# Chunked attention into a Swish feed-forward on one Trainium2 core: one more unit on each transfer-transpose path, and the order of the blocks around it

## The chip, the core and the metric

The kernel runs on one core of a Trainium2 chip. The core has five engines that run side by side: TensorE (PE, with its weight loads shown apart as PEld), VectorE (DVE), ScalarE (ACT), GpSimd (POOL, which here mostly issues loads) and SyncE (SP, which here issues stores and transposing transfers). Each engine works through its own list of instructions in order; an instruction that waits holds up all that stand behind it on that engine. The metric is the device time of one execution in microseconds (us).

## The reference

Attention within chunks of 64 tokens (8 batches, 8 heads, 576 tokens, head width 64), then a feed-forward with a Swish of its own slope for every hidden column:

```python
scores = scale * np.matmul(q_c, k_c.transpose(0, 1, 2, 4, 3))   # chunks of 64 x 64
attn = np.exp(scores - max); attn = attn / (sum + 1e-09)
x = np.matmul(attn, v_c)  -> [4608, 512]
h = x @ w_in                                                    # [512, 2048]
g = h * (1.0 / (1.0 + np.exp(-beta * h)))
out = g @ w_out                                                 # [2048, 512]
```

## The kernel before, in words

The 4608 tokens are cut into 18 **units** of 256 tokens and 9 **blocks** of two units each. Blocks 0 and 1 take units 0 to 3, block 2 takes units 4 and 5, block 3 takes 6 and 7, block 4 takes 8 and 9, and so on.

**Attention, unit by unit.** `load_qk` and `load_v` (lines 98 to 123) load q, k and v with GpSimd, cast to half precision. `emit_T` (line 152) turns q and k so that the head width lies on the partitions. For units below `XU` that is done by two DVE transposes (line 164), kT and qT. From `XU` on it is two transposing transfers issued by SP (line 159), and the loads then use another layout (line 106: two loads of 128 rows for q and two for k where line 112 has one each of 256 rows). `emit_T` also lets GpSimd issue loads up to four units ahead, and those wait for a free buffer of q and k (four of each). `emit_sc` (line 210) makes the scores: 64 small matmuls (line 232) for units below `XU`, 32 (line 219) from there on, then one ACT exponential. `emit_pv` (line 244) multiplies by v, `emit_norm` (line 301) divides on DVE and leaves x of half a unit, called x16. x must then be turned as well: `emit_xt_pe` (line 324) does half a unit with four PE transposes (line 329) and an ACT copy (line 333); `emit_xt_dma` (line 346) does it with a transposing transfer on SP (line 348). In the kernel before, units 0 to 5 go by the PE and units 6 to 17 by transfers.

**Feed-forward, block by block.** `emit_m(j, m)` makes one of the 16 column groups of the hidden layer of block j: four matmuls of 512 columns into a PSUM tile hps (line 372), an ACT tanh into sg (line 384), and a DVE instruction that makes gt from both (line 360). It reads the turned x of all four half units of its block. The second matrix product uses seven products of half size for four quarters; `emit_prod(j, p, t)` is half t of product p, eight matmuls of 256 columns (line 585), accumulated in one of two PSUM tiles; products 1, 6, 7, 4 go to the first and 2, 5, 3 to the second. The finished quarter is copied by ACT (line 602) or added by DVE (line 605). DVE also makes the sums that these products need: `emit_sum` (line 436) from gt, `emit_wt` (line 427) from the weights. In block j the core runs the first layer of block j and the products of block j-1, with the attention of later units between.

In blocks 6 to 8 the first layer too uses seven products for three quarters of its columns: `emit_q` (line 491), whose results are copied (line 503, ACT), added (line 506, DVE), put through Silu (`emit_q_silu`, line 513, three parts of two ACT instructions) and scaled into gt (`emit_q_scale`, line 527, DVE). The other four groups are `emit_m` with a Silu (line 381) and `emit_mg` (line 356, DVE).

**PSUM.** In block 2 the pool of four `p` buffers holds the two accumulators of block 1's products, so that two are left for hps: an `emit_m` needs the gt of the one two places before it. From block 3 on the accumulators are two tiles of their own, ya and yb.

**Order.** The order is written by hand: for every block a list of items (place, priority, what) is sorted by place and then priority (lines 738 to 801), and each engine gets its instructions in that order. An item's place is a share of the block.

Of the kernel before, what the change touches and what calls it, by code (L numbers as in the profile page):

```python
# [8 lines left out]
FP32 = mybir.dt.float32  # L9
# [6 lines left out]
def kernel(  # L16
# [59 lines left out]

    blocks = [(u, 2) for u in range(0, NU, 2)]
    NB = len(blocks)
    XU = 9
    WV = 8  # L80
    QB = 6
    unit_block = {}
# [469 lines left out]
    def emit_prod(j, p, t):  # L552
        last = j == NB - 1
        if p == 1 and t == 0:
            if j == 1:
                a = [ps_p[0].tile([128, 512], FP32, tag="p", name="acc") for _ in range(2)]
            else:
                a = [ps_y[0].tile([128, 512], FP32, tag=n, name=n) for n in (("yb", "ya") if last else ("ya", "yb"))]
            if last:
                a = [[ps_p[0].tile([128, 512], FP32, tag="p", name="acc") for _ in range(2)], a]  # L560
            acc_t[j] = a
        g = gt_t[j]
        acc = acc_t[j][0 if p in (1, 6, 7, 4) else 1]
        acc, dst = (acc[t][:, 0:256],) * 2 if last else (acc, acc[:, 256 * t:256 * t + 256])
        c0 = t * 128
        for kk in range(8):
            lhsT = {
                1: lambda: g[:, kk, c0:c0 + 128],
                2: lambda: g[:, 8 + kk, c0:c0 + 128],
                3: lambda: sm[3][:, kk, c0:c0 + 128],  # L570
                4: lambda: g[:, 8 + kk, 256 + c0:256 + c0 + 128],
                5: lambda: sm[0][:, kk, c0:c0 + 128],
                6: lambda: sm[1][:, kk, c0:c0 + 128],
                7: lambda: sm[2][:, kk, c0:c0 + 128],
            }[p]()
            rhs = {
                1: lambda: w_at(0, kk, 0),
                2: lambda: w_at(1, kk, 0),
                3: lambda: w_at(1, kk, 1),
                4: lambda: wt[3][:, kk, :],  # L580
                5: lambda: wt[0][:, kk, :],
                6: lambda: wt[1][:, kk, :],
                7: lambda: wt[2][:, kk, :],
            }[p]()
            nc.tensor.matmul(  # L585
                out=dst,
                lhsT=lhsT,
                rhs=rhs,
                start=(p in (1, 2, 5) and kk == 0 and (t == 0 or last)),
                stop=(kk == 7 and (t == 1 or last)),  # L590
                skip_group_check=True,
            )
        if t == 0 and not last:
            return
        flush_stores()
        r, c, how = {1: (0, 0, "copy"), 2: (0, 0, "add"), 6: (0, 1, "copy"), 5: (1, 1, "copy"),
                     7: (1, 1, "add"), 3: (0, 1, "add"), 4: (1, 0, "copy")}[p]
        key = (j, r, c, t if last else None)
        if how == "copy":
            o = osl_p[0].tile([128, 256], FP32, name="osl") if last else osb_p.tile([128, DM], FP32, tag="osb", name="osb")  # L600
            oq_t[key] = o
            nc.scalar.copy(out=o, in_=acc)  # L602
        else:
            o = oq_t[key]
            nc.vector.tensor_tensor(out=o, in0=acc, in1=o, op=ALU.add)
        if p in (2, 7, 3, 4):
            late.append(key)
# [6 lines left out]
    with tc.manual_schedule():  # L614
# [104 lines left out]
        def att_items(u, a0, w):  # L719
            it = [(a0, 2, ("sc", u)), (a0 + 0.36 * w, 3, ("pv", u)), (a0 + 0.361 * w, 3, ("norm", u, 0)),  # L720
                  (a0 + (0.42 if u >= WV else 0.50) * w, 3, ("norm", u, 1))]
            if u >= WV:
                it.append((a0 + (0.45 * w if u == 9 else 0.005), 3, ("T", u + 3)))
            return it

        ATT = {2: ((6, 0.36, 0.27), (7, 0.60, 0.27)),
               3: ((8, 0.01, 0.30), (9, 0.28, 0.30), (10, 0.66, 0.33)),
               4: ((11, 0.02, 0.33), (12, 0.35, 0.33), (13, 0.68, 0.33)),
               5: ((14, 0.02, 0.30), (15, 0.30, 0.30), (16, 0.58, 0.30), (17, 0.86, 0.28))}
# [8 lines left out]
        for j in range(1, NB):  # L738
# [6 lines left out]
            items = []  # L745
            if j == 1:
                items += [(0.04 * m, 0, ("h", m)) for m in range(8)]
                items += [(0.32 + 0.0850 * (m - 8), 0, ("m", m)) for m in range(8, KFF)]
                items += [(0.30, 3, ("T", 4)), (0.52, 2, ("sc", 4)), (0.70, 2, ("pv", 4)), (0.71, 3, ("norm", 4, 0)),
                          (0.80, 3, ("norm", 4, 1)), (0.56, 3, ("Th", 5, "kT")), (0.63, 3, ("Th", 5, "qT"))]  # L750
                items += [(c, 3, ("wt", i)) for i, c in ((1, 0.47),)]
            else:
                m0 = {2: 0.36, 4: 0.09}.get(j, 0.02)
                if j < QB:
                    items += [(m0 + (1 - m0) * m / KFF, 0, ("m", m)) for m in range(KFF)]
                else:
                    lane = LANE[2 if j == QB else j == NB - 1]
                    cost = [1 if it[0] == "q" and it[2] == 3 else 2 for it in lane]
                    for n, it in enumerate(lane):
                        c, e, f = (0.98 * sum(cost[:n + d]) / sum(cost) for d in (0, 1, 2))  # L760
                        items.append((c, 0, it))
                        if it[0] == "m":
                            items.append((c + 0.04, 3, ("mg", it[1])))
                        elif it[0] == "last":
                            pass
                        elif it[2] == 2:
                            if j == NB - 1 and it[1] == 3:
                                f = e
                            items += [(f - 0.002, 2, ("qs", it[1], 2)), (f - 0.001, 2, ("qs", it[1], 1)),
                                      (f + 0.03, 3, ("qt", it[1], 0))]  # L770
                        elif it[2] == 3:
                            items += [(c + 0.001, 2, ("qs", it[1], 0)), (c + 0.04, 3, ("qt", it[1], 1))]
                    if j == QB:
                        items.append((0.01, 6, ("open",)))
                        items += [(0.011+0.001*n, 6, ("tx", QB, n)) for n in range(4)]
                    if j + 1 < NB:
                        items += [(0.70 + 0.06 * n, 5, ("tx", j + 1, n)) for n in range(4)]
# [5 lines left out]
                    for i, c in ((2, 0.72), (0, 0.80), (1, 0.86)):  # L783
                        items.append((c, 4, ("pre", i)))
                for i in range(4):
                    s0 = (0.01, 0.08, 0.25, 0.33)[i] if j == 2 else 0.005 + 0.07 * i
                    if j >= QB:
                        s0 = (0.08, 0.15, 0.33, 0.48)[i] if j == QB else (0.003, 0.10, 0.33, 0.48)[i]
                    items.append((s0, 4, ("sum", i)))
                if j == 2:  # L790
                    items += [(c, 3, ("wt", i)) for i, c in ((2, 0.36), (3, 0.55))]
                    items += [(0.03, 0, ("sc", 5)), (0.06, 2, ("xp", 4, 0)), (0.09, 2, ("xp", 4, 1)),
                              (0.17, 2, ("pv", 5)), (0.18, 3, ("norm", 5, 0)), (0.19, 3, ("norm", 5, 1)),
                              (0.24, 3, ("T", 6)), (0.53, 3, ("T", 7)), (0.60, 3, ("T", 8)), (0.61, 3, ("T", 9)), (0.80, 3, ("T", 10)),
                              (0.30, 2, ("xp", 5, 0)), (0.32, 2, ("xp", 5, 1))]
                for jw, i, c, d in ((3, 2, 0.10, 0.22), (4, 1, 0.21, 0.22), (4, 3, 0.10, 0.22)):
                    if jw == j:
# [4 lines left out]
            for _, _, it in items:  # L802
# [13 lines left out]
                    emit_pv(it[1], (0, 1) if len(it) == 2 else (it[2],))  # L816
                elif it[0] == "norm":
                    emit_norm(it[1], it[2])
                    if it[1] not in (4, 5):
                        emit_xt_dma(it[1], it[2])  # L820
                elif it[0] == "xp":
                    emit_xt_pe(it[1], it[2])
# [68 lines left out]
```

## Time and profile before

| what | before |
|---|---|
| time, median of 3 runs (lowest to highest) | 276.55 us (276.26 to 276.83) |
| the profiled execution's own time | 276.39 us |
| its span, first to last instruction | 274.6 us |
| TensorE's granted clock | full in all slices |
| transposing transfer of x (line 348), 24 of them, median issue to landing | 6.6 us |
| transposing transfers of k and of q (line 159), 9 of each, median | 9.3 and 9.8 us |
| block 2, from its first product to the first of block 3 | 62.90 to 94.83 us |

The difference between the profiled execution's time and its span, 1.8 us, lies around the program's instructions. Times of single events below are counted from the start of the span. In the lists of instructions a row has the start, the time, the engine, the line, the operation, the tile written and the tiles read, how many instructions are merged, and in brackets how long the engine had been idle and what ended it.

### The profile page before, as it was taken

Reading aid. Unit: us, or ns where it says so; the run is one execution under the profiler, and the core shown is the slowest. Engines: PE = TensorE matmul, PEld = TensorE weight load, DVE = VectorE, ACT = ScalarE, POOL = GpSimd, SP = SyncE. Lnnn points to the kernel's source line nnn. Section 1 sums busy time; section 2 is a strip of 40 time slices with the busy share of each in tenths; the row PEclk is TensorE's granted clock in tenths of the full one; section 3 lists DMA queues with packets and bytes.
Section 4 is the critical chain, followed back from the end, with each engine's and each line's share of the span. In section 5 each row is a group of like instructions: output and inputs, shape, how many; then the busy total and the mean of one; then the engine's idle time right before and its main releaser. Section 6 shows DMA issues by size and latency. Waiting matters only on the chain.

```text
span 274.6 us, 7824 instructions
## 1 busy us (share of the span) xinstructions
PE 266.6 (97%) x3237; PEld 184.8 (67%) x3237; DVE 210.0 (76%) x394; ACT 166.8 (61%) x300; POOL 95.2 (35%) x122
## 2 busy tenths in 40 slices
PE   7799999999999999999999999999999999999995
PEld 2575445847665666666666666668887887778874
DVE  3567666899998598678977896759896977777961
ACT  2388416976664565556655655576768495858721
POOL 8954478489639935333445200000000000000000
PEclk9999999999999999999999999999999999999999
DMA  9999999999999999999999999853111102110223
GB/s 137 170 195 203 190 181 187 235 171 172 173 149 168 171 174 153 176 146 146 158 153 195 133 137 197 183 147 80 41 54 60 41 0 79 38 41 1 78 79 115
DMA packets 141763, 36.43 MB, mean 133 GB/s; under 512 B 125856, under 2 KB 141216, under 8 KB 141728
## 3 DMA queue, kind: packets, MB, share of 16 engines
q0 software_dynamic: 99136, 18.10, 83.3%
q1 hardware_dynamic: 42592, 17.84, 35.7%
q8 instruction: 25, 0.41, 0.6%
q14 instruction: 10, 0.08, 0.1%
HBM read 36.71 MB, written 9.44 MB: 168 GB/s over the span
## 4 chain that ended last, share of the span: by engine, by line
PE 78%; DVE 10%; ACT 5%; issue 3%; DMA 2%; POOL 0%; DVEq 0%; ACTq 0%; POOLq 0%
PE hps L372 28%; PE ya L585 14%; PE yb L585 11%; PE ops L397 5%; PE acc L585 5%; PE qx L484 4%; PE qz L484 4%; DVE gt L360 3%; ACT hq L513 3%; DMA sm<-in_k_dram 2%; DVE gt L527 2%; PE sc L232 2%; DVE sm L436 1%; PE sc L219 1%; PE x L270 1%
## 5 line engine op out<-in xcount | busy, mean ns | idle before, releaser
L372 PE MATMUL hps<-xt,win 128*128 128x512 f16 (+1 forms) x488 | 106.5, 355 | 0.5 <-DVE gt L360 0.3
L384 ACT ACTIVATE sg<-hps,bt 128x512 f32<-128x512 f32 (+1 forms) x111 | 69.3, 635 | 35.0 <-PE hps L372 32.6
L360 DVE SCALAR_TENSOR_TENSOR gt<-sg,hps 128x512 f16<-128x512 f32 (+1 forms) x111 | 67.6, 617 | 27.7 <-ACT sg L384 26.8
L372 PEld LDWEIGHTS <-win 128*128 128x128 f16 x488 | 46.2, 98 | 32.1 <-issue 1.0
L585 PEld LDWEIGHTS <-sm 128*128 128x128 f16 x512 | 49.4, 98 | 12.0 <-issue 0.3
L585 PEld LDWEIGHTS <-gt 128*128 128x128 f16 x384 | 36.9, 98 | 10.3 <-DVE gt L527 0.8
L120 POOL DMA_DIRECT2D vbig<-in_v_dram x40 | 34.0, 864 | 24.8 <-DMA ku<-in_k_dram 7.4
L585 PE MATMUL ya<-wt,sm 128*128 128x256 f16 x200 | 25.9, 273 | 0.0
L527 DVE TENSOR_SCALAR gt<-hq,rb 128x512 f16<-128x512 f32 x36 | 16.3, 483 | 8.4 <-ACT hq L513 7.2
L106 POOL DMA_DIRECT2D qu<-in_q_dram x20 | 17.1, 872 | 14.1 <-DVE qT L164 5.8
L106 POOL DMA_DIRECT2D ku<-in_k_dram x20 | 17.1, 880 | 12.2 <-DMA qu<-in_q_dram 7.8
L513 ACT ACTIVATE hq<-hq,bs 128x256 f32<-128x256 f32 (+1 forms) x36 | 19.2, 612 | 1.8 <-DVE hq L506 1.8
L436 DVE TENSOR_TENSOR sm<-gt 128x2048 f16<-128x2048 f16 (+1 forms) x17 | 19.7, 1156 | 0.3
L602 ACT COPY osb<-ya 128x512 f32<-128x512 f32 x18 | 10.6, 589 | 8.6 <-PE ya L585 7.9
L484 PEld LDWEIGHTS <-ws 128*128 128x128 f16 x144 | 14.1, 98 | 2.4 <-issue 0.7
L241 ACT ACTIVATE et<-sc 128x1024 f16<-128x1024 f32 (+1 forms) x10 | 8.3, 852 | 11.4 <-PE sc L232 11.4
L397 PE MATMUL ops<-wout,gt 128*128 128x512 f16 x64 | 14.7, 379 | 0.0
L585 PE MATMUL yb<-wout,gt 128*128 128x256 f16 x104 | 13.9, 273 | 0.3 <-DVE gt L527 0.2
L585 PE MATMUL yb<-wt,sm 128*128 128x256 f16 x104 | 13.5, 273 | 0.1
L503 ACT COPY hq<-qx 128x512 f32<-128x512 f32 x18 | 10.6, 587 | 4.9 <-PE qx L484 4.8
L585 PE MATMUL ya<-wout,gt 128*128 128x256 f16 x104 | 13.5, 273 | 0.0
L585 PE MATMUL yb<-wout,sm 128*128 128x256 f16 x104 | 13.5, 273 | 0.0
(99 smaller groups left out, 355.7 us busy)
## 6 DMA issues: line engine op xcount, KB each, us to landing
out_dram<-osb SPq DMA_DIRECT2D x32, 256.0 KB, 2.8
vbig<-in_v_dram POOLq DMA_DIRECT2D x32, 128.0 KB, 7.5
qu<-in_q_dram POOLq DMA_DIRECT2D x18, 128.0 KB, 12.5
ku<-in_k_dram POOLq DMA_DIRECT2D x18, 128.0 KB, 14.6
win<-in_moe_w_in_dram POOLq DMA_DIRECT2D x8, 256.0 KB, 8.7
wout<-in_moe_w_out_dram POOLq DMA_DIRECT2D x4, 512.0 KB, 13.2
qu<-in_q_dram POOLq DMA_DIRECT2D x5, 256.0 KB, 7.0
ku<-in_k_dram POOLq DMA_DIRECT2D x5, 256.0 KB, 7.1
```

The costliest lines, as they stand in the source:

```text
L106: nc.gpsimd.dma_start(out=tv[off:off + n, sp], in_=src[b, :, s:s + n, :].rearrange("h p d -> p h d"),)
L120: nc.gpsimd.dma_start(out=vbig[off:off + n, i % NV, :, 0:D], in_=v[b, :, s:s + n, :].rearrange("h p d -> p h d"),)
L360: nc.vector.scalar_tensor_tensor(out=gt_t[j][:, m, c0:c0 + n], in0=sg[:, 0:n], scalar=1.0, in1=hps[:, 0:n], op0=ALU.add, op1=ALU.mult,)
L372: nc.tensor.matmul(out=hps[:, 0:n], lhsT=w_in16[m // 2][:, kk, (m % 2) * 128:(m % 2) * 128 + 128], rhs=xr[:, c0 // CH:(c0 + n) // CH, 2 * ...
L384: nc.scalar.activation(out=sg[:, 0:n], in_=hps[:, 0:n], func=ACTF.Tanh, scale=bt[:, m:m + 1])
L397: nc.tensor.matmul(out=ops, lhsT=gt_t[j][:, kk, t * 128:(t + 1) * 128], rhs=w_out16[kk // 4][:, kk % 4, :], start=(kk == 0), stop=(kk == K ...
L436: nc.vector.tensor_tensor(out=sm[i][:, lo:hi, :], in0=a, in1=b, op=op)
L484: nc.tensor.matmul(out=dst[:, s, :], lhsT=lhsT, rhs=rhs, start=(p in (1, 2, 5) and s == 0 and kk == 0), stop=(s == 1 and kk == 1), skip_gr ...
L503: nc.scalar.copy(out=o, in_=z if p == 5 else x)
L513: nc.scalar.activation(out=o, in_=src, func=ACTF.Silu, scale=bs[:, m:m + 1])
L527: nc.vector.tensor_scalar(out=gt_t[j][:, m, :], in0=hq[:, b].rearrange("p c q -> p (c q)"), scalar1=rb[:, m:m + 1], scalar2=None, op0=ALU. ...
L585: nc.tensor.matmul(out=dst, lhsT=lhsT, rhs=rhs, start=(p in (1, 2, 5) and kk == 0 and (t == 0 or last)), stop=(kk == 7 and (t == 1 or last ...
```

## The change

Five edits, all in the order or in which path a unit takes.

1. `XU` is 8 in place of 9: q and k of unit 8 are loaded in the other layout and turned by two transfers on SP, and its scores take 32 matmuls.
2. x of unit 4 is turned by two transfers behind its two norms; the two items `xp 4` are gone from block 2.
3. Orders in blocks 1 and 2. In block 1 only `T 4` moves, ahead of the half group `h 7`. In block 2: `sc 5` goes behind the second half of product 1; `sum 3` goes behind `m 0` and `sc 6`, `wt 2` behind `m 1`, `wt 3` behind `sc 7`; `T 8` goes ahead of `m 4` and `T 7` (it stood behind `sc 7`); `pv 7` with the first norm of unit 7 goes behind `prod 3 0` and `m 9`, and the second norm behind `m 10` and `prod 3 1`.
4. In blocks 6 to 8 the Silu parts of a q group: part 2 goes one item of the lane earlier, and in blocks 6 and 7 the last group's parts 2 and 1 go ahead of `m 3`, its first scaling ahead of `prod 4 1`.
5. The two accumulators change places from block to block (yb first in even blocks, ya first in odd ones), where before only the last block had them the other way.

```diff
-    XU = 9
+    XU = 8
...
-                a = [ps_y[0].tile([128, 512], FP32, tag=n, name=n) for n in (("yb", "ya") if last else ("ya", "yb"))]
+                a = [ps_y[0].tile([128, 512], FP32, tag=n, name=n) for n in (("ya", "yb") if j % 2 else ("yb", "ya"))]
...
-        ATT = {2: ((6, 0.36, 0.27), (7, 0.60, 0.27)),
+        ATT = {2: ((6, 0.36, 0.27), (7, 0.60, 0.36)),
...
-                items += [(0.32 + 0.0850 * (m - 8), 0, ("m", m)) for m in range(8, KFF)]
-                items += [(0.30, 3, ("T", 4)), (0.52, 2, ("sc", 4)), (0.70, 2, ("pv", 4)), (0.71, 3, ("norm", 4, 0)),
-                          (0.80, 3, ("norm", 4, 1)), (0.56, 3, ("Th", 5, "kT")), (0.63, 3, ("Th", 5, "qT"))]
+                items += [(0.34 + 0.0820 * (m - 8), 0, ("m", m)) for m in range(8, KFF)]
+                items += [(0.26, 3, ("T", 4)), (0.52, 2, ("sc", 4)), (0.70, 2, ("pv", 4)), (0.715, 3, ("norm", 4, 0)),
+                          (0.75, 3, ("norm", 4, 1)), (0.56, 3, ("Th", 5, "kT")), (0.63, 3, ("Th", 5, "qT"))]
...
-                            if j == NB - 1 and it[1] == 3:
+                            if it[1] == 3:
                                 f = e
-                            items += [(f - 0.002, 2, ("qs", it[1], 2)), (f - 0.001, 2, ("qs", it[1], 1)),
+                            items += [(e - 0.002, 2, ("qs", it[1], 2)), (f - 0.001, 2, ("qs", it[1], 1)),
                                       (f + 0.03, 3, ("qt", it[1], 0))]
...
-                    s0 = (0.01, 0.08, 0.25, 0.33)[i] if j == 2 else 0.005 + 0.07 * i
+                    s0 = (0.01,0.08,0.28,0.36)[i] if j == 2 else 0.005 + 0.07 * i
...
-                    items += [(c, 3, ("wt", i)) for i, c in ((2, 0.36), (3, 0.55))]
-                    items += [(0.03, 0, ("sc", 5)), (0.06, 2, ("xp", 4, 0)), (0.09, 2, ("xp", 4, 1)),
+                    items += [(c, 3, ("wt", i)) for i, c in ((2, 0.40), (3, 0.60))]
+                    items += [(0.07, 2, ("sc", 5)),
                               (0.17, 2, ("pv", 5)), (0.18, 3, ("norm", 5, 0)), (0.19, 3, ("norm", 5, 1)),
-                              (0.24, 3, ("T", 6)), (0.53, 3, ("T", 7)), (0.60, 3, ("T", 8)), (0.61, 3, ("T", 9)), (0.80, 3, ("T", 10)),
+                              (0.24, 3, ("T", 6)), (0.53, 3, ("T", 7)), (0.50, 3, ("T", 8)), (0.61, 3, ("T", 9)), (0.80, 3, ("T", 10)),
                               (0.30, 2, ("xp", 5, 0)), (0.32, 2, ("xp", 5, 1))]
...
-                    if it[1] not in (4, 5):
+                    if it[1] != 5:
                         emit_xt_dma(it[1], it[2])
```

## The prediction

> **What bounds the kernel.** I read the page's busy times first, then busy times by stretch, then which PE starts were late.
>
> ```profile
> span 274.6 us, 7824 instructions
> PE 266.6 (97%) x3237; PEld 184.8 (67%) x3237; DVE 210.0 (76%) x394; ACT 166.8 (61%) x300; POOL 95.2 (35%) x122
> ...
> DMA  9999999999999999999999999853111102110223
> ```
>
> PE is the bound: only what takes PE time away, or a moment in which PE waits, can shorten the span. The transfer engines are full for the first 25 of 40 slices (to 172 us). By stretch (total, then busy us of PE, PEld, DVE, ACT, POOL):
>
> ```profile
> 51.60:75.40 23.80, 23.54 (x427) 15.64 (x428) 23.44 (x41) 16.81 (x29) 18.24 (x22) 1.00 2.07 177
> 75.40:96.50 21.10, 20.65 (x309) 12.80 (x294) 16.51 (x30) 11.74 (x17) 16.71 (x21) 1.00 2.18 162
> 96.50:185.00 88.50, 88.50 (x1146) 57.17 (x1145) 68.78 (x131) 54.03 (x91) 24.54 (x30) 1.00 1.55 162
> ```
>
> From 51.6 to 75.4 DVE is as full as PE (23.44 of 23.80), so PE time saved there is kept only if DVE lets it. From 96.5 to 185 PE never waits: what is won or lost before 96.5 goes straight through to the end. The late starts that the change touches:
>
> ```profile
> 64.20 0.71 PE L232 MATMUL sc<-qT,kT 32*64 32x64 f16 x64 [0.26 <-DVE x L313]
> ...
> 89.64 1.02 PE L372 MATMUL hps<-xt,win 128*128 128x512 f16 x4 [0.34 <-DVE gt L360]
> ...
> 213.74 0.60 PE L484 MATMUL qz<-tx,ws 128*128 128x256 f16 x4 [0.18 <-DVE hq L506]
> ```
>
> Ends of PE rows are modelled, so I count from start to start: a product half takes 0.87, a full `m` 0.86. By that 64.20 is 0.43 late, 89.64 0.50, and 213.74 and its twin at 238.93 0.34 each.
>
> **Part A, x of unit 4 and the order up to sc 7.** Removed: eight PE transposes (64.84 to 65.08 and 65.95 to 66.17, 0.46 in all) and two ACT copies (0.58 and 0.62). Scores of unit 5, which waited for unit 4's second norm (ended 64.15), go behind another product half, so the 0.43 shrinks to the usual change of shape, 0.09. PE could be 0.8 ahead. But DVE's list stays: gt to 65.33, two sums to 67.86, unit 5's norms to 69.54. PE's transpose of unit 5's second half started at 69.60 and will again: the 0.8 becomes a wait there. What is left is that one ACT copy instead of two stands between it and `m 0`: 70.70 in place of 70.82. Then `m 4`, its tanh, its gt and unit 7's two DVE transposes set sc 7: 81.00 in place of 81.06. Part A: 0.06.
>
> Cover: unit 4's transfers must land by 70.7. They start at 62.7 and 64.2; transfers of x while the loads run, in three stretches (77 to 81, 86 to 91, 104 to 108):
>
> ```profile
> DMA to landing us min/median/max: 4.9/5.4/5.8
> ...
> DMA to landing us min/median/max: 5.7/5.9/6.0
> ...
> DMA to landing us min/median/max: 8.6/8.8/8.9
> ```
>
> At 4.9 to 6.0 the second lands at 69.1 to 70.2: hidden. At 8.9, 73.1: rival 3. `T 4` ahead of `h 7` delays that group's gt by 1.3, with four hps buffers still in use: nothing.
>
> **Part B, unit 8's transposes leave DVE.** kT and qT took DVE from 82.70 to 83.99. Walking DVE's new list (gt 0.68, add 0.65, norm 0.92; tanh 0.69 begins 0.2 after its matmuls) from sc 7 at 81.0: gt 9 ends 87.6, unit 7's first norm 88.5, gt 10 89.1, product 3's add 89.7, second norm 90.5, gt 11 91.1. `m 12` needs gt 10 and PE is there at 89.06: the 0.50 goes. `m 13` needs gt 11 and PE is there at 90.9: a new 0.2. Part B: 0.30. The sums and weights that move later (sum 3, wt 2, wt 3) stay ahead of the products that read them.
>
> **Part C, 32 scores for 64.** By the PE rows, unit 8 took 95.80 to 96.49, 0.69; unit 9, already in the new form, 104.88 to 105.25:
>
> ```profile
> 95.80 0.71 PE L232 MATMUL sc<-qT,kT 32*64 32x64 f16 x64
> 96.49 0.81 PE L372 MATMUL hps<-xt,win 128*128 128x512 f16 x3
> ...
> 104.88 0.45 PE L219 MATMUL sc<-qT,kT 64*64 64x64 f16 x32
> 105.25 1.04 PE L372 MATMUL hps<-xt,win 128*128 128x512 f16 x4
> ```
>
> 0.69 - 0.37 = 0.32. So block 3's `m 0` is wanted at 96.49 - 0.06 - 0.30 - 0.32 = 95.81.
>
> **Part D, x of unit 7 is later.** That `m 0` reads unit 7's turned x. Before, the second norm ended 88.99, the transfer started 89.02 and landed 6.03 later, at 95.05: 1.4 to spare. Now the norm ends at 90.5 (part B). The second transfers of the two pairs took 4.88 and 6.03; I take their mean, 5.45: it lands at 95.98, `m 0` starts at 96.03, and of 0.68 remain 0.46. Both ends: 4.88 costs nothing, 6.03 leaves no gain, 8.9 is rival 2.
>
> SP's list in front of it grows: unit 8's kT and qT stand where unit 9's stood, unit 9's behind them.
>
> ```profile
> 77.58 2.63 SPq L348 DMA_TRANSPOSE xt<-x  x2
> 80.39 1.23 SPq L159 DMA_TRANSPOSE kT<-ku  x1
> 81.72 1.80 SPq L159 DMA_TRANSPOSE qT<-qu  x1
> 86.80 3.41 SPq L348 DMA_TRANSPOSE xt<-x  x2
> ```
>
> Unit 8's issue by 83.4 and unit 9's, at the longest such rows (2.5 and 4.1 to 4.3), by 90.2; at the shortest by 86.5. Unit 7's first half is ready at 88.5, its second at 90.5: the gap 83.5 to 86.8 covers it, just. Unit 8's own transfers are wanted at 95.4, ten us on. GpSimd issues four loads of 0.9 for unit 8 in place of two, 1.8 later for units 9 and 10; its 4.39 of idle time before 81.31 takes that up.
>
> The Trainium skill's page "DMA: Bandwidth & Descriptors", section "Latency and other measured facts", gives a transposing transfer 261 GB/s; as an estimate from that page, half a unit (131 KB) takes 0.50 us, and unit 7 would land at 91.0, leaving all 0.68. The rows of 4.9 to 8.9 beside the loads, and 2.4 to 2.6 after them, speak against sizing it so.
>
> **Part E, blocks 6 and 7.** The 213.74 wait comes down a chain: ACT's Silus start at 207.99, behind `m 3`'s Silu and a copy.
>
> ```profile
> 206.69 0.69 ACT L381 ACTIVATE sg<-hps,bs 128x512 f32<-128x512 f32 x1 [2.79 <-PE hps L372]
> 207.99 2.13 ACT L513 ACTIVATE hq<-hq,bs 128x256 f32<-128x256 f32 x4
> 209.54 1.89 DVE L527 TENSOR_SCALAR gt<-hq,rb 128x512 f16<-128x512 f32 x4 [1.64 <-ACT hq L513]
> 211.47 1.23 DVE L436 TENSOR_TENSOR sm<-gt 128x2048 f16<-128x2048 f16 x1
> ```
>
> In the new order they start when DVE's adds end (205.75) and fill ACT's 2.79 of idle time. The sum at 211.47 then starts at 210.55, and the 0.34 goes. What is late next: `m 3`'s Silu, at 207.9 in place of 206.7, so its gt ends 209.10; product 1, started at 208.60, reads it in its fourth matmul at 208.93 and waits 0.22. The osb copy also slips, and the change of places of ya and yb covers that, since product 1 no longer writes the tile being copied. Gain 0.34 - 0.22 = 0.12 per block (ends: -0.3 and +0.34), 0.24 for two.
>
> **Part F, block 8.** Silus of group 2 start 0.8 earlier in ACT's idle stretch before 251.23; DVE's second scaling, released by ACT at 253.85, can follow the first at 253.74. I take 0.14 (ends 0 and 0.27, the PE wait at 264.43 that hangs on it).
>
> **Sum.** 0.46 + 0.24 + 0.14 = 0.84, in the profiled execution: 276.39 - 0.84 = 275.55. That execution lay 0.16 under the median of the runs, so the median is 276.55 - 0.84 = 275.7.
>
> **Rivals.**
> 1. *Unit 7's x lands at its old 6.0 or up to 1 later.* 96.53 + 0.05 against 96.49: parts A to C are used up, 0.38 remains, to a loss of 0.6: 276.2 to 277.2; I write 276.5. For it: the nearest row is 6.03. Against: that row shared the engines with loads that may sit elsewhere now.
> 2. *Slower: unit 9's transfers are still queued when unit 7's come.* Place: block 3's first `m`. Behind unit 11's transfers, issued until 104.63, x of unit 8 took 8.9. So 90.5 + 8.9 = 99.4, `m 0` 2.9 late, less 0.38: 276.55 + 2.5 = 279.1. It decides once unit 9's qT is issued later than about 88.5; below a landing of 97.4 the total is not slower by 0.55. Against: the gap from 83.5 to 86.8.
> 3. *Unit 4's x lands late*, 73.1 for 70.7: 2.4 less 0.84: 278.1. Against: no other transposing transfer is in flight there.
> 4. *The engines are simply full.* 0.8 MB more in transposing transfers (half a unit of x is 131 KB, q or k of a unit 262 KB) shifts all loads behind it; unit 16's q landed 167.3 for scores at 171.51, 4.2 to spare. At 6 late PE waits 2: 277.7. The Trainium skill, same page, section "Issuing engines are not separate DMA queues", says that transfers of all issuing engines interleave on the same 16 engines; by that rule the shift is real, and the trace agrees: 2.4 alone, 8.9 beside loads.
> 5. *Part E turns round*: `m 3`'s gt later by another 0.4 costs 0.8 in two blocks: 276.5.
>
> **Chances.** Forecast 0.42 (its own range 275.2 to 276.2), rival 1 0.20, rival 2 0.16, rival 3 0.08, rival 4 0.06, rival 5 0.08. A measurement of this kernel tells about 0.2%, 0.55 us, from no change. Faster: 0.37 of the forecast and 0.03 of rival 5, 0.40. Same: 0.05 of the forecast, 0.16 of rival 1, 0.05 of rival 5, 0.26. Slower: 0.04 of rival 1 and rivals 2 to 4, 0.34. The range leaves out most of rival 2 above (a latency over 8) and 0.05 below: 275.1 to 278.2.
>
> **What will show it.** No start at 64.20 with a wait, but one at unit 5's transpose near 69.6 (A); no wait of `m 12`, a small one of `m 13` (B); 0.37 for unit 8's scores (C); the landing of unit 7's second half against block 3's first `m`, which decides most (D); Silus of the third group at 205.8 and 230.9, product 1's fourth matmul late by 0.2 (E). I am wrong if block 3's first `m` waits more than 0.7, or if any wait appears between 96.5 and 185.

## The result, and the profile after

The changed kernel takes 284.04 us (median of 6 runs, 282.94 to 285.04) against 276.76 us (6 runs of the kernel before beside them): a ratio of 1.026, interval 1.0245 to 1.0279, slower by 7.3 us. The profiled execution took 283.62 us. Times of whole kernels below are medians over all executions, and ratios compare averages without executions that were over 1.5% longer than the fastest of the same kernel (one of four with `pv 7` at its old place, two of ten with unit 8's transfers alone). Waits are read in one profiled execution of each kernel, whose own time is given where it lies far from the median.

First the head of the page of the changed kernel and its clock row.

```profile
span 281.8 us, 7751 instructions
...
PE 266.6 (95%) x3197; PEld 184.4 (65%) x3197; DVE 208.4 (74%) x392; ACT 166.2 (59%) x298; POOL 97.3 (35%) x124
...
PEclk9999999999999989999999999999999999999999
```

PE has 40 matmuls fewer and is busy for as long as before (266.6 us), in a span longer by 7.2 us. So PE stood still for longer somewhere, and where the clock row has its only 8 (99 to 106 us) its matmuls were slower. PE's timeline, start and time first, then what ran and what ended an idle time, has two new waits:

```profile
73.54 1.02 PE L372 MATMUL hps<-xt,win 128*128 128x512 f16 x4 [2.04 <-DMA xt<-x]
...
97.96 0.45 PE L219 MATMUL sc<-qT,kT 64*64 64x64 f16 x32
102.45 1.44 PE L372 MATMUL hps<-xt,win 128*128 128x512 f16 x4 [4.05 <-issue]
```

They are the first `m` of block 2 and the first `m` of block 3. From start to start the first is 2.20 late, the second 4.12 (the scores ahead of it take 0.37, as unit 9's did before). Both read a turned x. SP's own list, the issues of stores and transposing transfers (start, how long the issue held SP):

```profile
63.37 2.64 SPq L348 DMA_TRANSPOSE xt<-x  x2
...
83.03 2.03 SPq L159 DMA_TRANSPOSE kT<-ku  x1
85.16 1.25 SPq L159 DMA_TRANSPOSE qT<-qu  x1
86.58 2.88 SPq L159 DMA_TRANSPOSE kT<-ku  x1
89.55 2.51 SPq L159 DMA_TRANSPOSE qT<-qu  x1
92.15 1.37 SPq L348 DMA_TRANSPOSE xt<-x  x1
93.57 0.73 SPq L539 DMA_DIRECT2D out_dram<-osb  x1
94.39 1.56 SPq L348 DMA_TRANSPOSE xt<-x  x1
```

x of unit 4 is the first row: issued at 63.37 and 64.81, it landed at 70.03 and 73.41, 6.66 and 8.60 later. The second half stands so in the chain of work that ended last (start, time, what):

```profile
64.81 8.60 DMA xt<-x
73.41 0.14 issue
```

x of unit 7 is in the last rows of SP's list. Its norms end with these two rows of DVE:

```profile
90.46 0.69 DVE L313 TENSOR_TENSOR x<-x,rd 128x512 f16<-128x512 f32 x1
...
92.49 0.69 DVE L313 TENSOR_TENSOR x<-x,rd 128x512 f16<-128x512 f32 x1
```

They ended at 91.15 and 93.18, but SP was still issuing unit 9's qT until 92.06, then the first half, then a store that was next in SP's list, so the second half went out at 94.39, 1.2 after its norm. It landed 7.97 later, at 102.36, and `m 0` starts at 102.45. The time from issue to landing of those two halves, shortest, median and longest:

```profile
DMA to landing us min/median/max: 7.5/7.7/8.0
```

The clock by stretches around the second wait (columns: total, busy time and count of PE, PEld, DVE, ACT, POOL, granted clock, transfer engines, GB/s):

```profile
100.00:102.00 2.00, 0.00 (x0) 0.00 (x0) 0.00 (x0) 0.00 (x0) 0.41 (x1) 1.00 1.57 171
102.00:104.00 2.00, 1.55 (x6) 0.73 (x7) 0.00 (x0) 0.07 (x1) 0.88 (x1) 0.73 1.61 158
104.00:106.00 2.00, 2.00 (x10) 1.27 (x9) 1.35 (x2) 0.98 (x2) 0.69 (x1) 0.50 1.75 157
106.00:108.00 2.00, 2.00 (x44) 1.20 (x42) 0.83 (x2) 0.91 (x2) 1.06 (x2) 0.92 1.76 187
```

From 102 to 108 the missing clock is (0.27 + 0.50 + 0.08) x 2.0 = 1.7 us. The starts of the matmuls say the same: between 100 and 110 PE loses 6.0 against its usual spacing, of which 4.1 are the wait and 0.2 were lost there before.

**The sum.** 2.2 (first wait) + 4.1 (second wait) + 1.7 (clock) + 0.7 (PE was this much later by 20 us already, in code that is the same; profiled executions differ there by up to 1.3) - 1.5 (what the edits save, worked out below) = 7.2, the difference of the two profiled executions (283.62 - 276.39 = 7.23).

### The profile page after: what moved, and what is told of

It is laid out like the page before. It is cut to its first block, busy times and chain, and to the rows that moved or that the text cites. A ratio compares the mean times of both kernels' runs of the same rounds, so it can differ in the third digit from the quotient of the medians.

```text
span 281.8 us, 7751 instructions
## 1 busy us (share of the span) xinstructions
PE 266.6 (95%) x3197; PEld 184.4 (65%) x3197; DVE 208.4 (74%) x392; ACT 166.2 (59%) x298; POOL 97.3 (35%) x124
## 4 chain that ended last, share of the span: by engine, by line
PE 75%; DVE 9%; DMA 8%; POOL 3%; issue 2%; ACT 2%; DVEq 0%; POOLq 0%
PE hps L372 28%; PE ya L585 13%; PE yb L585 13%; PE qx L484 5%; PE qz L484 4%; PE acc L585 3%; PE ops L397 3%; DMA xt<-x 3%; DMA qu<-in_q_dram 3%; DMA ku<-in_k_dram 2%; DVE gt L360 2%; DVE sm L436 2%; PE sc L219 1%; DVE x L313 1%; POOL vbig L120 1%
## 5 line engine op out<-in xcount | busy, mean ns | idle before, releaser
L106 POOL DMA_DIRECT2D ku<-in_k_dram x22 | 18.7, 863 | 15.9 <-DMA qu<-in_q_dram 11.8
L513 ACT ACTIVATE hq<-hq,bs 128x256 f32<-128x256 f32 (+1 forms) x36 | 19.9, 609 | 5.5 <-DVE hq L506 5.5
L106 POOL DMA_DIRECT2D qu<-in_q_dram x22 | 18.6, 855 | 12.3 <-DMA vbig<-in_v_dram 4.4
L585 PE MATMUL yb<-wt,sm 128*128 128x256 f16 x152 | 19.7, 273 | 0.1
L585 PE MATMUL ya<-wt,sm 128*128 128x256 f16 x152 | 19.7, 273 | 0.0
L585 PE MATMUL yb<-wout,gt 128*128 128x256 f16 x104 | 14.8, 284 | 0.2
L241 ACT ACTIVATE et<-sc 128x1024 f16<-128x1024 f32 (+1 forms) x9 | 7.3, 833 | 10.4 <-PE sc L232 10.3
L506 DVE TENSOR_TENSOR hq<-qz,hq 128x512 f32<-128x512 f32 x18 | 12.3, 683 | 1.1 <-ACT hq L503 0.8
L278 DVE TENSOR_TENSOR x<-x,rx 128x512 f16<-128x512 f32 (+1 forms) x20 | 11.9, 620 | 0.3
```

What stands on the lines that cost most here:

```text
L106: nc.gpsimd.dma_start(out=tv[off:off + n, sp], in_=src[b, :, s:s + n, :].rearrange("h p d -> p h d"),)
L506: nc.vector.tensor_tensor(out=o, in0=x if p == 7 else z, in1=o, op=ALU.add)
L513: nc.scalar.activation(out=o, in_=src, func=ACTF.Silu, scale=bs[:, m:m + 1])
L585: nc.tensor.matmul(out=dst, lhsT=lhsT, rhs=rhs, start=(p in (1, 2, 5) and kk == 0 and (t == 0 or last)), stop=(kk == 7 and (t == 1 or last ...
```

## The experiments

Unless a text says otherwise each starts from the changed kernel. Medians of the kernel before, beside them, were 276.8 to 276.95.

### One part undone

**x of unit 4 by PE again.**

```diff
-(0.07, 2, ("sc", 5)),
+(0.07, 2, ("sc", 5)), (0.06, 2, ("xp", 4, 0)), (0.09, 2, ("xp", 4, 1)),
...
-                    if it[1] != 5:
+                    if it[1] not in (4, 5):
```

> The changed kernel with x of unit 4 turned by the PE again (eight PE transposes, 0.46 us), all else as changed. Theory: the loss is two waits for a transfer of x, 2.20 us in block 2 (unit 4) and 4.23 us in block 3 (unit 7) with about 1.3 us of slow clock behind it. Then the first wait goes, its 2.2 less 0.5 is won, and the second stays near 4: 284.0 - 1.7 = 282.3. Rival: the transfer engines are simply over-full and the delay is only moved; then unit 7's wait grows by as much and the time stays at 284.

281.62 us, ratio 1.018 (1.0145 to 1.0216). (The 4.23 of this expectation counts from the last of the scores; by their usual length it is the 4.12 above.) The first wait is gone. Block 3's `m 0` waited 5.86 in the profiled execution (283.69, the longest of four; the others took 281.4 to 281.7), and the clock stood at 0.50 from 100 to 106. PE got there 2.5 earlier, x of unit 7 landed only 0.7 earlier: SP issued unit 9's qT until 91.8. The first loss belongs to unit 4's transfer alone, the second does not need it.

**`pv 7` at its old place.**

```diff
-        ATT = {2: ((6, 0.36, 0.27), (7, 0.60, 0.36)),
+        ATT = {2: ((6, 0.36, 0.27), (7, 0.60, 0.27)),
```

> The changed kernel with the second half of unit 7's attention at its old place in block 2, 1.7 us earlier. If the late norm sets unit 7's landing, block 3's first product comes 1.7 us earlier: 282.3, wait 2.5. If SP's queue sets it (unit 9's transfers are issued until 92.06, before unit 7's), the norm can be early and the transfer is not: gain under 0.7, 283.3 or more.

282.41 us, ratio 1.016 (1.0114 to 1.0206). In the profiled execution (279.74, the shortest of four) the second wait fell from 4.05 to 1.65. The second norm ended 1.8 earlier there (91.37), its transfer left 1.9 earlier (92.50, still 1.1 behind its norm) and landed at 100.18, 2.2 earlier: the late norm counts, by about as much as was expected for it. And `m 12` waits 0.34 again (0.50 from start to start), although unit 8's DVE transposes are still gone:

```profile
90.65 1.03 PE L372 MATMUL hps<-xt,win 128*128 128x512 f16 x4
92.02 1.02 PE L372 MATMUL hps<-xt,win 128*128 128x512 f16 x4 [0.34 <-DVE gt L360]
```

So what removed that wait is the other place of unit 7's norms. The same move makes unit 7's x later.

**Unit 9's transfers behind unit 7's x.**

```diff
-(0.61, 3, ("T", 9))
+(0.785, 3, ("T", 9))
```

> The changed kernel with unit 9's two transposing transfers issued behind both of unit 7's x. If SP's queue and the transfers ahead in it are what made unit 7's x late, its two halves start when their norms end (91.2 and 93.2), land some 6 us later (97 to 99.2), the wait in block 3 falls from 4.2 to under 1, the slow clock behind it goes, and the time is 284.0 - 4.5 = 279.5. If the late norm or the loads set it, the landing stays at 101 or later and the time above 282.5. Unit 9's scores are wanted at 112.5 before; they should still find their data.

280.22 us, ratio 1.011 (1.0081 to 1.014). The best of the single edits to the changed kernel, 3.8 us. The wait before block 3 is still 2.42: the second half of unit 7's x left when its norm ended (93.65), but still took 7.53, only 0.44 less than with unit 9's transfers ahead of it. So what this edit wins is the early issue more than a shorter transfer. The clock stayed at 1.00 here, which it did not in the changed kernel.

**Unit 8 on DVE again**, x of unit 4 the only added transfer.

```diff
-    XU = 8
+    XU = 9
...
-(0.50, 3, ("T", 8))
+(0.60, 3, ("T", 8))
```

> The changed kernel, but unit 8's q and k are again transposed by DVE (scores in 64 small matmuls), so x of unit 4 is the only added transfer. Theory (unit 4's x is late by itself, because its second transfer takes about 8.6 us beside the loads; unit 7's x is late because unit 9's and unit 8's transposing transfers are ahead of it on SP): block 2's first m still waits about 2.1 us near 73.5; block 3's first m waits 0 to 0.5; median 276.8 + 2.1 - 0.5 (parts A and E) = 278.4. Rival (unit 4's x is late only because SP or the engines carry unit 8's transfers too): no wait at 73.5, median 276.3. Rival (the later second norm of unit 7 alone makes its x late): block 3's first m still waits over 2 us, median over 280.

281.96 us, ratio 1.017 (1.013 to 1.0217); the profiled execution, 284.06, was the longest of five. The first theory got only its first half right.

```profile
73.09 1.87 PE L372 MATMUL hps<-xt,win 128*128 128x512 f16 x4 [2.28 <-DMA xt<-x]
...
102.83 1.43 PE L372 MATMUL hps<-xt,win 128*128 128x512 f16 x4 [3.14 <-DMA xt<-x]
```

Unit 4's x is late by itself. But unit 7's x is late without unit 8's transfers too. SP was free from 86.6. It issued the first half at 92.21, when its norm was done, and the second at 94.98, 0.8 after its own, behind the first and a store: with the changed order and unit 8's transposes on DVE, the second norm ends at 94.2, 5.5 before `m 0` asks for its data, where the kernel before has 7.5. It then took 7.77, although SP had been free. The rival (the later norm is enough) holds; why the transfer took 1.7 longer than before is not shown.

### One part alone, put into the kernel before

**Unit 8's transfers alone.**

```diff
-    XU = 9
+    XU = 8
...
-(0.60, 3, ("T", 8))
+(0.50, 3, ("T", 8))
```

> The kernel before with one part of the change: unit 8's q and k transposed by transfers, issued at place 0.50 of block 2 as in the changed kernel. All of blocks 1 and 2 otherwise as before, x of unit 4 by PE. Theory (unit 9's transfers stand on SP ahead of unit 7's x, and SP is held until about 92): unit 7's second norm ends near 88.5, but its transfer is issued near 93 and lands near 101; block 3's first m waits about 5 us and PE's clock falls after it (1.3 us); median 276.8 - 0.8 + 5 + 1.3 = 282.3 (280.5 to 283). Rival (the later second norm, from the other order in blocks 1 and 2, is what makes unit 7's x late): x lands near 95, no wait, median 276.0.

280.84 us, ratio 1.012 (1.0092 to 1.0152). SP and then PE in the profiled execution (279.41):

```profile
85.00 1.50 SPq L159 DMA_TRANSPOSE kT<-ku  x1
86.61 3.03 SPq L159 DMA_TRANSPOSE qT<-qu  x1
89.73 3.62 SPq L348 DMA_TRANSPOSE xt<-x  x2
```

```profile
99.09 1.02 PE L372 MATMUL hps<-xt,win 128*128 128x512 f16 x4 [2.05 <-DVE sm L436]
```

The second norm ended at 89.8 and its transfer went out at 91.80, 2.0 late, behind unit 9's and its own first half. It landed at 99.00, which is what `m 0` waited for: the bracket names a DVE sum because a wait for several semaphores is put down to one of them. The wait is 2.1 from start to start in this execution, not 5, but its place and its cause are as expected. Unit 9's transfers on SP are enough by themselves, and so is the later norm. In the changed kernel they meet.

**x of unit 4 by transfers alone**, the scores of unit 5 at their old place.

```diff
-(0.03, 0, ("sc", 5)), (0.06, 2, ("xp", 4, 0)), (0.09, 2, ("xp", 4, 1)),
+(0.03, 0, ("sc", 5)),
...
-                    if it[1] not in (4, 5):
+                    if it[1] != 5:
```

> The kernel before with one part of the change: x of unit 4 by transfers, the scores of unit 5 at their old place, unit 8 by DVE. Theory: the transfers are issued near 62.7 and 64.2 and the second lands 8.6 us later, 72.8, against block 2's first m at 70.4: a wait of 2.4 and a lower clock behind it (about 0.5 us); everything after it is later by as much, so unit 7's x is still in time; median 276.8 + 2.5 = 279.3 (278.8 to 279.9). Rival (the late landing belongs to the other order of the changed kernel): no wait over 0.5, median 276.4.

279.89 us, ratio 1.010 (1.0064 to 1.0134): +3.0 us. In the profiled execution block 2's `m 0` waited 2.02, the clock fell to 0.50 behind it, and unit 7's x is in time.

**The same with more work in front of block 2's first `m`.**

```diff
-                m0 = {2: 0.36, 4: 0.09}.get(j, 0.02)
+                m0 = {2: 0.50, 4: 0.09}.get(j, 0.02)
```

> The same kernel (x of unit 4 by transfers alone), with block 2's first m at place 0.50 in place of 0.36: two product halves and the scores of unit 6 run in front of it, about 2.4 us. Theory (only the order decides whether the transfer is hidden): the wait before block 2's first m goes to 0 to 0.4; the m's then stand closer together, and what the eight transposes cost is saved (0.46): median 276.3 to 277.3, at least 1.5 under the run with the transfers at the old order. Rival (products or the m's wait for DVE or ACT instead): a wait over 1 us elsewhere between 70 and 96, median 278 or more.

278.43 us, ratio 1.006 (1.004 to 1.0076). The wait for x and the slow clock behind it are gone and 1.5 us are won back, but new waits stand there, from start to start 0.70 before the scores of unit 6 (for qT, late on DVE) and 0.91 before an `m` (for its gt). The order can hide the transfer; it then pays elsewhere, and the eight transposes saved do not make up for it.

**The edits of blocks 6 to 8 alone.**

```diff
-... for n in (("yb", "ya") if last else ("ya", "yb"))]
+... for n in (("ya", "yb") if j % 2 else ("yb", "ya"))]
...
-                            if j == NB - 1 and it[1] == 3:
+                            if it[1] == 3:
...
-                            items += [(f - 0.002, 2, ("qs", it[1], 2)), ...
+                            items += [(e - 0.002, 2, ("qs", it[1], 2)), ...
```

> The kernel before with only the two edits for blocks 6 to 8: the Silu parts earlier and the two accumulators changing places. Theory: both waits of 0.34 us in blocks 7 and 8 go, a new one of 0.0 to 0.22 comes at product 1, the end gains 0 to 0.3: 276.76 - 0.5 = 276.3 (276.0 to 276.6). Rival: these edits cost (a late gt of the last plain group): 277.0 or more.

276.57 against 276.95 us, ratio 0.9984 (0.9969 to 0.9998): a small gain, about 0.4 us.

### The clock

```diff
+                if j == 3:
+                    items.append((0.015, 0, ("idle", 18)))
...
+                elif it[0] == "idle":
+                    emit_idle(it[1], 512)
```

> The changed kernel with 18 matmuls of 512 columns on zeros put between the scores of unit 8 and block 3's first m (18 x 0.216 = 3.9 us, about the 4.2 us that PE waits there). They do nothing for the output. Theory (the idle PE loses clock for some us after the wait, which costs 1.3 to 2 us on top of it): the granted clock stays at 0.99 or 1.00 from 100 to 110, block 3's first m starts within 0.5 us of 102.4, and the median is 282.7, 1.3 us under the changed kernel (284.0). Rival (the slow rows after the wait come from the loads or from something else): the clock falls all the same, median 284.0 or above.

281.6 us, ratio 1.017 (1.013 to 1.0214), 2.4 less than the changed kernel. (The tile that the added matmuls read is shared with a sum of weights, so they ran on those and not on zeros.) The same stretches as above:

```profile
102.00:104.00 2.00, 2.00 (x11) 0.88 (x9) 0.00 (x0) 0.00 (x0) 0.88 (x1) 1.00 1.61 157
104.00:106.00 2.00, 2.00 (x14) 1.18 (x12) 0.82 (x2) 1.27 (x2) 0.87 (x1) 1.00 1.83 156
106.00:108.00 2.00, 2.00 (x45) 1.42 (x44) 2.00 (x6) 0.69 (x1) 0.92 (x2) 1.00 1.68 156
```

x landed no earlier (103.11) and `m 0` started at 103.39. Work that is thrown away in the wait kept the clock at 1.00 there, and the time fell: the slow stretch was PE's idleness, not the loads. The mean clocks over whole executions agree: 0.982 to 0.994 in the six of the changed kernel, 0.999 or 1.000 in three of the four here (the fourth, the profiled one at 282.86, fell to 0.50 once behind block 2's wait).

### Why unit 4's x takes 8.6 us

**The loads issued after it held back** (units 9 and 10, until unit 5's x is in place).

```diff
-        loads_to(u + 4)
+        if u not in (5, 6):
+            loads_to(u + 4)
...
+(0.33, 3, ("late",))
...
+                elif it[0] == "late":
+                    nc.gpsimd.tensor_copy(out=braw[:, 0:1], in_=xt_t[2][:, 3, 0, 0:1])
+                    loads_to(10)
```

> The changed kernel with the loads of units 9 and 10 held back on GpSimd until x of unit 5 is in place (a copy of one column on GpSimd that reads it, near 70.8): no load is issued from about 65.3 to 70.8, five in the changed kernel. Theory (x of unit 4 is late because it shares the 16 engines with the loads issued after it): its second transfer lands 5 to 6 us after its issue, 69 to 70.5, and block 2's first m waits 0 to 0.5; block 3's first m still waits 4 us or more; median 284.0 - 2.2 = 281.8. Rival (the loads issued before it, or the transfer's own speed, set the 8.6): it lands at 8 us or more and the wait of 2 us stays, median 283.5 or more.

284.57 us, ratio 1.028 (1.026 to 1.0309). The transfers took 6.6 and 8.4, the wait stayed. The theory fell.

**The loads of unit 8 held back too**, so that GpSimd issues none from 60.8 to 71.9:

```diff
-        if u not in (5, 6):
+        if u not in (4, 5, 6):
```

> As the last run, but the loads of unit 8 are held back too: GpSimd issues no load from about 59.5 to 70.8. Theory (x of unit 4 is late because the packets of loads issued before it are served first: its own packets appear in the trace only about 3 us after its issue): the second transfer lands within 3 to 5.5 us, 67 to 69.8, and block 2's first m waits 0 to 0.2. Units 8's to 10's q and k come later, so later waits may grow; median 280 to 284. Rival (the transfer's own speed, or what stops the engines near 71, sets it): it lands 8 us or more after its issue all the same, and the wait of 2 us stays.

The packets by queue from 64.7 to 66.1 us, first in the run with the loads of unit 8 in place, then without (software_dynamic: GpSimd's loads; hardware_dynamic: SP's transfers), and the landing of unit 4's two halves in the second:

```profile
q0 software_dynamic: 1718, 0.22, 242.6%
```

```profile
q1 hardware_dynamic: 752, 0.18, 84.8%
q0 software_dynamic: 260, 0.03, 36.4%
```

```profile
DMA to landing us min/median/max: 3.3/3.7/4.1
```

x was issued at the same time in both (62.9 and 63.1 for the first half). With loads in front of it, not one of its packets moves in that window; without, most of them do. Its halves land 3.3 and 4.1 us after their issue and block 2's first `m` does not wait. So the 8.6 comes from the loads of unit 8, issued from 60.8 to 66.1 in the changed kernel and for the most part ahead of it. The whole kernel takes 287.67 us, ratio 1.039 (1.0368 to 1.0409): with the loads pushed back SP issues unit 9's transfers until 95.03, ahead of unit 7's x, and block 3's `m 0` waits 8.84.

### Versions without the two waits

**Unit 8's transfers, unit 9's behind unit 7's x, the edits of blocks 6 to 8**, the rest as before. (The edits of blocks 6 to 8 as above.)

```diff
-    XU = 9
+    XU = 8
...
-(0.60, 3, ("T", 8)), (0.61, 3, ("T", 9))
+(0.50, 3, ("T", 8)), (0.785, 3, ("T", 9))
```

> The kernel before with unit 8's q and k by transfers, unit 9's transfers moved behind unit 7's x (place 0.61 to 0.785), and the edits of blocks 6 to 8 (order of the Silus and places of ya and yb). Theory: unit 7's x is issued when its norms end (about 87.5 and 88.5) and lands 5 to 7.5 us later, 94 to 96, against block 3's first m at 95.7; block 2's first m does not wait; median 276.8 - 0.8 (no DVE transposes, 32 scores) - 0.4 (Silus) + 0 to 0.7 = 275.6 to 276.3. Rival (a full set of transfer engines makes x take 8 us or more whatever is ahead on SP): m waits over 1.5 us, median 277.2 or more.

276.39 us, ratio 0.9997 (0.9972 to 1.0023). No wait at either `m`. The 0.50 of `m 12` is back, and in the profiled execution a unit far behind waited for its q, as it had not in the kernel before:

```profile
172.55 0.45 PE L219 MATMUL sc<-qT,kT 64*64 64x64 f16 x32 [1.03 <-DMA qT<-qu]
```

**The changed kernel with unit 4 by PE, unit 9's transfers later, and block 3's first `m` later.**

```diff
-                m0 = {2: 0.36, 4: 0.09}.get(j, 0.02)
+                m0 = {2: 0.36, 3: 0.15, 4: 0.09}.get(j, 0.02)
...
-(0.07, 2, ("sc", 5)),
+(0.07, 2, ("sc", 5)), (0.06, 2, ("xp", 4, 0)), (0.09, 2, ("xp", 4, 1)),
...
-(0.61, 3, ("T", 9))
+(0.785, 3, ("T", 9))
...
-                    if it[1] != 5:
+                    if it[1] not in (4, 5):
```

> The changed kernel with x of unit 4 by PE again, unit 9's transfers behind unit 7's x (place 0.785), and block 3's first m moved behind two more product halves and the values of unit 8 (place 0.02 to 0.15, about 2.2 us). Theory (both losses are places where PE asks for a turned x too early; what the change saves elsewhere is real): neither block 2's nor block 3's first m waits over 0.3, the granted clock stays at 1.00, and the median is 276.8 - 0.32 (scores) - 0.5 (the wait of m 12) - 0.4 (blocks 6 to 8) = 275.6 (275.3 to 276.1). Rival (the transfers shift the loads, and a later unit waits for its q as unit 16 did in one profile): a wait of 1 us or more between 140 and 175, median 276.6.

277.9 us, ratio 1.005 (1.0018 to 1.0076). In the profiled execution (279.53) both `m` start without a wait, but unit 9's transfers, pushed behind, are now late for unit 9's scores:

```profile
104.96 0.44 PE L219 MATMUL sc<-qT,kT 64*64 64x64 f16 x32 [2.42 <-DVE gt L360]
```

Its qT was issued from 93.99 to 97.73 and landed at 104.82 (the bracket again names another of several), and the clock fell to 0.50 behind that wait. The expectation missed: the wait moved on.

**The second norm of unit 7 behind gt 10**, once with unit 8's transfers and unit 9's behind (as two runs above), once with none of the added transfers; both with the edits of blocks 6 to 8.

```diff
-(0.42 if u >= WV else 0.50) * w
+(0.42 if u >= WV else 0.61 if u == 7 else 0.50) * w
```

> The run with unit 8's transfers, unit 9's behind unit 7's x and the late Silus, with one edit more: the second norm of unit 7 goes behind gt 10 on DVE (place 0.735 to 0.765). Theory (that norm, and not DVE's transposes of unit 8, makes m 12 wait): the 0.50 wait near 89.9 falls to 0 to 0.2; the norm ends about 0.7 later, its transfer lands near 95.5 to 96.2 against block 3's first m at 95.7, a wait of 0 to 0.5; median 275.7 to 276.4. Rival (m 12 waits for something else): 0.50 stays, median 276.4 to 277.

> The kernel before with the edits of blocks 6 to 8 and the second norm of unit 7 behind gt 10 (place 0.735 to 0.765); no added transfer, unit 8 by DVE. Theory: m 12's wait of 0.50 falls to 0 to 0.2, gt 11 comes 0.7 later and m 13 waits 0 to 0.4; unit 7's x lands near 95.8 of the 96.5 at which block 3's first m is wanted, no wait; median 276.8 - 0.4 (blocks 6 to 8) - 0.1 to 0.5 = 275.9 to 276.3. Rival (the wait only moves on to m 13): median 276.4, the same as the Silu edits alone.

275.86 us, ratio 0.9976 (0.9957 to 0.9994), and 275.99 us, ratio 0.9967 (0.9954 to 0.9979). In neither does `m 12` or `m 13` wait. DVE in the second of them:

```profile
89.03 0.69 DVE L360 SCALAR_TENSOR_TENSOR gt<-sg,hps 128x512 f16<-128x512 f32 x1 [0.69 <-ACT sg L384]
89.89 0.69 DVE L360 SCALAR_TENSOR_TENSOR gt<-sg,hps 128x512 f16<-128x512 f32 x1 [0.18 <-ACT sg L384]
90.50 0.20 DVE L307 RECIPROCAL rd<-x 128x8 f32<-128x8 f32 x1
90.73 0.69 DVE L313 TENSOR_TENSOR x<-x,rd 128x512 f16<-128x512 f32 x1
```

gt 10 (89.89) now starts as soon as its tanh is there, and the norm (90.50 to 91.42) follows. Its x landed at 97.13, and block 3's `m 0` did not wait for it. Both versions beat the kernel before by 0.2 to 0.3%, and the changed kernel by 2.9%. The one without added transfers gains as much: the scores' 0.32 could not be seen in the time.

## Why the prediction was wrong

The forecast was 275.7 in a range that ended at 278.2; 284.0 lies far outside. The gains came (1.45 in the profiled execution, where the parts without D had 1.06), though not all for the reason given; both covers that the forecast relied on gave way, and a third loss was not in it.

**Part A: the cover of unit 4's transfers, the first step that failed.** The transfers were taken as hidden at a latency of 4.9 to 6.0; the second took 8.60 and landed at 73.41, for an `m` that could have started at 71.34. The argument was that no other transposing transfer is in flight there. The runs show that this is not enough: the loads in front of it set the latency (8.4 with them, 4.1 without). 4.9 to 6.0 was read in other stretches, without asking what stood in front of x there; the row at 8.8, put aside for rival 3, was the size to take. The rest of part A came as written: the wait before unit 5's scores shrank to 0.09, PE waited 0.55 at unit 5's second half near 70.2 instead, and 0.15 was left (0.06 forecast).

**Part B: right in kind (0.50 for 0.30), wrong in its reason.** The 0.50 of `m 12` went, and the 0.2 of `m 13` did not come. But DVE's transposes of unit 8 were not its cause: without them and with the norms at their old places it stayed in three runs, and with them and the second norm moved it went. The walk along DVE's list had both edits in it and gave the whole gain to one of them.

**Part C: right.** Unit 8's scores are one row of 0.45 at 97.96, as unit 9's were before, and in the run that fills the wait the next matmul starts 0.38 behind them, for 0.69 before.

**Part D: the step that decides, off by 3.9 us.** It had `m 0` wait 0.2; it waited 4.1. The second norm was forecast for 90.5. It ended at 93.18, which is 90.5 once the 2.7 are taken off by which the scores of unit 7 were later than forecast (83.71 for 81.00): right. From the end of that norm to the place where `m 0` asks for its x there were 7.5 us before, 5.3 by the forecast and 5.1 as measured. Two terms were not right. First, "the gap covers it, just": SP was held by unit 9's transfers until 92.06 (89.3 on the same count), and the second half left 1.2 after its norm. Second, the latency, 7.97 for 5.45. The mean of two rows that had no unit 8 in front of them was the wrong size. With unit 9's transfers just ahead the second half took 7.2 to 9.1 in seven profiled runs, and with unit 9's behind it 5.4 and 6.2 in two, 7.5 in a third. But moving unit 9's transfers took only 0.4 off in the changed kernel, and with unit 8 on DVE and SP free it was 7.8 all the same. So that the issue is held by unit 9's transfers is shown; what makes this transfer itself slower stays open. 0.2 (forecast) + 1.2 (issue) + 2.5 (latency) + 0.2 (less time from norm to `m 0`) = 4.1.

**Rivals 2 and 3 both came true, and at once.** Their mechanisms and sizes were right. Rival 3 expected 2.4 and measured 2.2. Rival 2 expected a landing at 99.4; 102.36 less the 2.7 is 99.7. Here two errors nearly cancelled: the transfer left 1.2 later than its norm and took 0.9 less than the 8.9. The point from which rival 2 decides (unit 9's qT issued later than 88.5) was passed: 89.3 on the forecast's count here, and 89.6 in the run with unit 8's transfers alone, where `m 0` waited 2.1. The chances of 0.16 and 0.08 were summed as if only one could happen. 276.55 + 2.4 + 2.9 - 0.4 (what rival 2 leaves of the gains) would have given 281.5, outside the range, and 283.2 with the 1.7 of the clock.

**What was missing: the clock.** No case had a price for what PE loses after a long wait: 1.7 by the trace of the profiled execution, 2.4 between the medians in the run that fills the wait. The Trainium skill's page "TensorE: Matmul & The Clock Gate", section "Part 1: The HAM clock gate", says that PE's clock is halved after an idle window of about 3.4 us and comes back after as long a busy one. The 0.50 after the 4.05 agrees.

**Part E: right in kind, better than forecast.** The waits of block 6 and 7 fell by 0.24 each (0.12 forecast): only about 0.1 is left at product 1. **Part F** shows nothing: the waits near 264 are the same in kernels with and without it. Together 0.48, where the run of these edits alone measured 0.4 (0.38 forecast for both).

Gains in the profiled execution: 0.15 (A) + 0.50 (B) + 0.32 (C) + 0.48 (E) = 1.45.

**Rival 4** (loads shifted by the added bytes) showed once, as 1.03 before unit 16's scores in one version; the changed kernel has no wait between 110 and 185.

## What to carry to other kernels

What is queued ahead of a transfer when it is issued can double its time: count the loads of the last few microseconds and the transfers on the same issuing engine, and take the latency from a row with the same neighbours, the long one if in doubt (here 4.1 without loads in front and 8.4 with them). When a step is moved, its last consumer's slack shrinks from both ends (the producer ends later, the consumer asks sooner), and rivals that sit at different places add up. A wait of PE of two or three microseconds can cost more than itself: here the granted clock fell to 0.50 at the longer ones, for 3.4 us or a multiple of it, which is 1.7 us lost each time if PE is busy throughout.

## What the hardware showed that was not expected

**The clock.** After waits of 3.1 us and more (five in these profiles) the granted clock always fell to 0.50. After waits of 1.65 to 2.42 us it fell in five of eleven: not after the 2.04 of the changed kernel's block 2, but after 2.02 with x of unit 4 alone. By the clock records of these traces eight of the ten stretches at 0.50 that came with these waits lasted 3.41 or 3.42 us; the one at the wait of 5.86 lasted 6.83, and the one at 8.84 lasted 10.24, twice and three times as long. The Trainium skill's figure of 3.4 us of idleness, in the section named above, is no safe lower bound here; it also says that the window runs freely, and that equal waits end differently would fit that. Why 2 us of idleness are enough is not shown.

**Packets do not mix at once.** In the window shown above SP's transfers moved nothing for a good while beside GpSimd's loads: x issued at 62.9 had its first packets at 66.6, and with the loads of unit 8 gone x issued at 63.05 had them at 64.3. The Trainium skill's page "DMA: Bandwidth & Descriptors", section "Queues, rings and completion order", says that an engine goes round between the queues it has work for; by that, x's packets would have been mixed with the loads' from the start. The trace does not show that. Whether they waited at the engines or were not made yet can't be told from it.

**Empty stretches.** For about 1 us at a time the transfer engines move almost nothing while transposing transfers are under way. In the changed kernel, one stretch just ahead of the landing of unit 4's x:

```profile
71.00:72.00 1.00, 0.51 (x5) 0.20 (x3) 1.00 (x3) 0.71 (x2) 0.00 (x0) 1.00 0.21 9
```

9 GB/s, for 150 around it. Such stretches are in the kernel before too (81.75 to 83.0). In the profiles read for it, each came about 1 us after a 16 KB packet of the queue for instructions, and those packets had no such stretch behind them where no transposing transfer was under way. What links the two was not tried, and stays open; as an estimate, without the stretch unit 4's x would have been up to 1 us earlier, and still late.
